# Seven small transfers instead of three, so that the last store counts on the last semaphore waited for

## The chip, the cores and the metric

The kernel runs on 1 core of one Trainium2 chip. Its five engines are TensorE (PE in the profile, its weight loads PEld), VectorE (DVE), ScalarE (ACT), GpSimd (POOL) and SyncE (SP). SP computes nothing here: it starts most transfers between HBM and the on-chip memory. The metric is device time in microseconds (us) of one execution.

## The reference

Two stages over `x` of 4 batches, 11,456 tokens and 128 channels, all in float32.

```python
h = mab(I, x)            # 32 inducing points attend to all tokens of a batch
y = mab(x, h)            # every token attends to the 32 rows of h
xn = y / (norm(y) + 1e-6);  en = emb / (norm(emb) + 1e-6)
logits = xn @ en.T / tau                       # 8 experts
out = max(softmax(logits)) * relu(y @ w1[e]) @ w2[e],   e = argmax(logits)
```

`mab(q, kv)` is softmax(q kv^T / sqrt(128)) kv. Three inputs are small: the inducing points (`ind`, 16 KB), the experts' embeddings (`emb`, 4 KB) and one number, `tau`.

## The kernel before, in words

Each batch is cut into 6 pieces of 1,920 tokens, so there are 24 pieces. A piece is 960 KB in and 960 KB out. For a piece g the program has steps with names: `load g` (transposed layout) and sometimes `loadx g` (plain layout) bring it in, `xt`/`xe` transpose it on the chip where `loadx` does not, `s1`, `e1`, `e1t`, `h` do the first attention, `s2`, `am`, `e2`, `ud`, `w`, `n2`, `ln`, `ex`, `den`, `lg`, `el`, `S`, `v`, `gf` the second one and the gate, `F`, `eg`, `out`, `oe` the output, and `store g` writes it. Steps of a batch (`hd`, `tab`, `vote`, `pick`, `loadw`, `G`, `GT`, `gs`, `gk`, `K`) find its expert and fetch that expert's weights. The first piece is loaded in two halves, `load 0.0` and `load 0.1`; pieces 17, 18, 20, 22 and 23 are written in two halves.

The order of the work is written out by hand. `ORDER` (line 42) is one list of all steps; each engine runs its steps in that order. `AT` (line 99) is a string of digits: each time a step of the list touches a buffer for the first time, the next digit is its place (which of 18 big buffers, which of 8 PSUM banks). `FILL` (line 105) names steps before which TensorE multiplies zeros into a bank that is free: `out 17.1:2:1:w` is one multiplication of 512 columns into bank 2 ahead of `out 17.1`.

**Transfers and semaphores.** Each transfer counts on one of eight semaphores, DMAHW0 to DMAHW7, which are handed out in turn. The order of the turns is about that of the list, SP's and ACT's transfers mixed. Before a transfer may take a semaphore that an earlier one has, its engine waits until the earlier one has landed. So a row `[waits DMAHW3_49]` on a transfer says at once which semaphore it counts on (unless its buffer or the pace of the loads asks for that landing too) and that the transfer eight turns ago has to have landed. SP's loads are also paced: load number n of the list waits for load n - 6.

The three small inputs are started by ACT: `ind` (line 305) one transfer, `small` (line 307) one for `emb` and one for `tau`. With SP's 73 transfers that makes 76.

**The end.** The kernel checks bounds on its own shortcut (`verdict`), reads a count (line 810) and enters a loop (line 812) which repairs batches; the count is 0 here and no pass is made. Leaving that loop, each of the five engines passes the same row of waiting instructions: for DMAHW1 together with DMAHW0, then DMAHW2, DMAHW3, and so on to DMAHW7, then for the engines. After it the engines meet at a barrier, which GpSimd gathers, and a second one.

Of the kernel before, what the change touches and what calls it, by code (L numbers as in the profile page):

```python
# [23 lines left out]
E = 8  # L24
# [14 lines left out]
LOADED = [3, 6, 7, 8, 13, 14, 15, 16, 19, 20, 22]  # L39


ORDER = """load 0.0, load 0.1, ind, small, xt 0.0, s1 0, xt 0.1, xe 0.0, load 1, m1 0, xe 0.1, sha 0, xt 1.0, load 2, xt 1.1,
s1 1, s1 2, en1, en3, xe 1.0, shb 0, shc 0, xe 1.1, shd 0, e1 0, en4, e1t 0, xt 2.1, en5, load 4, xe 2.1, xt 2.0,
xe 2.0, xt 4.1, xt 4.0, en6, e1 1, e1 2, pz 0, e1t 1, py 0, h 0, load 3, s1 3, s1 4, e1t 2, h 1, h 2, e1 4, xe 4.1,
e1t 4, e1 3, xe 4.0, pad 5, e1t 3, load 5, s1 5, e1 5, zc 0, en7, xt 5.0, xt 5.1, loadx 3, load 6, xe 5.0, h 3,
# [50 lines left out]
store 22.0, eg 23.1, verdict.0, verdict.1, verdict.2, verdict.3, out 23.1, oe 22.1.1, store 22.1, verdict.4,  # L96
verdict.5, oe 23.1.0, oe 23.1.1, verdict, store 23.1"""

AT = """0024120363045430065602601011745018109021046abc00d10121324356ef0732g1h7210161000213400045617261a042030111013700
8114c060100463230010013150146003911364102117eh8360710c00216004006133145701011600421000b116240671d1452117502f90  # L100
645610014043141b006400201100016c402601101004509h23156000252410006101342015106200111401158006710262514a6106275c
24000g62111301103460010e02409101216430201301641d103101264130c010100420015062814502610254116211116010426404011g
2064a020416201f14012362460"""

FILL = """xt 0.0:6:17:n, tab 3:1:2:w, out 17.1:2:1:w, out 18.1:0:3:w, out 19:2:1:w, out 21:4:2:w, out 20.0:3:10:w,
out 23.0:5:2:w, out 22.0:5:1:w, ck4 3:6:1:w, out 23.1:7:2:w"""

BY_DVE = (
# [44 lines left out]
class Plan:  # L153
# [5 lines left out]
    def add(self, name, engines, f, reads=(), writes=()):  # L159

        part = lambda a: a if isinstance(a, tuple) else (a, None)
        op = Op(name, engines, f, [part(a) for a in reads], [part(a) for a in writes])
        for key in op.reads + op.writes:
            w, r = self.hist.setdefault(key, [None, []])
            if w is not None and w is not op:
                op.deps.add(w)
        for key in op.writes:
            op.deps.update(x for x in self.hist[key][1] if x is not op)
            self.hist[key] = [op, []]
        for key in op.reads:  # L170
            self.hist[key][1].append(op)
        op.bufs = list(dict.fromkeys(k[0] for k in op.reads + op.writes))
        for b in op.bufs:
            b.left += 1
        self.ops.append(op)
        return op

    def run(self):
        named = {op.name: op for op in self.ops}
        order = [named[n.strip()] for n in ORDER.split(",")]  # L180
        assert len(named) == len(self.ops) == len(order) == len(set(order))
        holds = {(k, s): None for k, n in SLOTS.items() for s in range(n)}
        at, done = iter("".join(AT.split())), set()
        for o in order:
# [17 lines left out]
def tile_attn_moe(ctx: ExitStack, tc: tile.TileContext, xT, xP, xR, indT, emb, tau, w1, w2, aux, outT):  # L202
    nc = tc.nc
# [17 lines left out]
    for kind, shapes in dict(  # L221
# [3 lines left out]
        w=dict(w1=[P, F], w2=[P, 8, C]),  # L225
# [9 lines left out]
    ident, ind, ones, iota = const("ident", [P, P]), const("ind", [P, M]), const("ones", [P, P]), const("iota", [P, E])  # L235
# [3 lines left out]
    en, itau, ess, nrm = const("en", [P, E]), const("itau", [E, 1]), const("ess", [E, P]), const("nrm", [E, 4])  # L239
    emb_sb = const("emb_sb", [E, P])  # L240
# [38 lines left out]
    add = plan.add  # L279
# [22 lines left out]
    cbuf, cnb = Buf("cst"), Buf("cst")  # L302
    enb, tb = Buf("cst"), Buf("cst")

    add("ind", {"ACT": (0.6, 16e3)}, lambda e: [nc.scalar.dma_start(ind, indT)], [], [cnb])

    def load_small(e):
        return [nc.scalar.dma_start(emb_sb, emb), nc.scalar.dma_start(itau, tau.broadcast_to([E, 1]))]

    add("small", {"ACT": (1.0, 5e3)}, load_small, [], [tb])  # L310

    def experts1(e):
# [432 lines left out]
    with tc.manual_schedule():  # L745
        nc.scalar.preload_act_table_set("natural_log_exp_and_others")
        constants()
        hist, last, paced = {}, {}, []
        fills = {n.strip(): (int(s), int(k), w == "w") for n, s, k, w in (x.split(":") for x in FILL.split(",") if x.strip())}
        for op in order:  # L750
            res = []
            for key in (op.reads, op.writes):
                out = []
# [9 lines left out]
            if op.name in fills:  # L763
                s, n, wide = fills[op.name]
                w, r = hist.setdefault(("ps", s), [None, []])
# [4 lines left out]
            for key in reads + writes:  # L770
                w, r = hist.setdefault(key, [None, []])
# [40 lines left out]
    with tc.For_i(0, n_left, 1) as b:  # L812
# [12 lines left out]
        xt, pe = tile_("xt", [P, GW]), tile_("pe", [M, GW])  # L825
        m1, nb1, fx, zc1 = (tile_(n, [M, 1]) for n in ("m1", "nb1", "fx", "zc1"))
# [26 lines left out]
        r1, r2, half, place, at_e = (tile_(n, [GW, 1]) for n in ("r1", "r2", "half", "place", "at_e"))  # L853
# [93 lines left out]
```

## Time and profile before

| | |
|---|---|
| median of 3 runs | 164.43 us (164.41, 164.43, 166.8) |
| the profiled execution's own time | 164.44 us |
| its span, first to last instruction | 162.6 us |
| granted TensorE clock over the span | 0.99 |
| PE, DVE, ACT, POOL busy | 151.5, 122.8, 113.6, 67.8 us |
| moved by transfers | 62.33 MB, 383 GB/s mean |

The span leaves out 1.9 us of the execution's time. A row of a timeline has the start and the length in us, engine, source line, operation, tiles and, in brackets, how long the engine was idle before and what ended the idling. An engine with a q behind its name is its sequencer: transfers being issued, semaphore waits and branches, which do not count as busy. Names such as `big` leave the buffer's number out.

### The profile page before, as it was taken

What the parts mean: (1) busy time and instruction counts of PE and PEld (TensorE: products, weight loads), DVE (VectorE), ACT (ScalarE), POOL (GpSimd) and SP (SyncE); (2) the same over time, 40 slices, a digit from 0 to 9 for tenths busy, and PEclk for the clock granted to TensorE, in tenths of its full rate; (3) what the DMA queues carried; (4) which work ended last, traced back from release to release, by engine and by line L of the source; (5) the groups of instructions that cost most, each with busy time, mean ns of one, the idle gap of its engine ahead of it and who ended that gap; (6) DMA issues with size and microseconds to landing.
All of it is one profiled execution on the core that took longest, in us unless ns stands there. A gap on an engine that the chain in (4) does not pass through costs nothing.

```text
span 162.6 us, 5452 instructions
## 1 busy us (share of the span) xinstructions
PE 151.5 (93%) x2130; PEld 85.3 (52%) x2134; DVE 122.8 (76%) x308; ACT 113.6 (70%) x249; POOL 67.8 (42%) x179
## 2 busy tenths in 40 slices
PE   7999999999999999999999999999999998998720
PEld 5769695335986633546487423658753223233300
DVE  0175743699978789999986598989898989996620
ACT  3239361683985888697678877699968879987740
POOL 8700010116266470524142552942456275775500
PEclk9999999999999999999999999999999999999995
DMA  5999999999999999999999989999999999879972
GB/s 165 428 429 420 429 422 427 407 315 423 422 416 429 423 386 415 425 418 421 429 416 368 403 295 310 381 427 427 416 419 422 322 420 401 343 302 421 405 294 97
DMA packets 10716, 62.33 MB, mean 383 GB/s; under 512 B 1336, under 2 KB 1344, under 8 KB 10688
## 3 DMA queue, kind: packets, MB, share of 16 engines
q1 hardware_dynamic: 10512, 61.94, 94.4%
q8 instruction: 17, 0.28, 0.6%
q14 instruction: 11, 0.09, 0.1%
q10 hardware_dynamic: 176, 0.02, 0.1%
HBM read 38.49 MB, written 23.46 MB: 381 GB/s over the span
## 4 chain that ended last, share of the span: by engine, by line
PE 83%; ACT 9%; POOL 2%; issue 1%; DVE 1%; ACTq 0%; POOLq 0%
PE psum L294 65%; PE psum L404 14%; ACT big L291 5%; PE psum L768 3%; PE psum L366 1%; ACT s L636 1%; POOL Wp L620 1%; ACT gf L653 1%; ACT U L291 1%; ACT E L601 1%; POOL E2g L677 0%; ACT s L637 0%; POOL lg L644 0%; DVE fl L709 0%; POOL chk L482 0%
## 5 line engine op out<-in xcount | busy, mean ns | idle before, releaser
L291 ACT COPY big<-psum 128x960 f32<-128x960 f32 (+4 forms) x71 | 57.4, 845 | 13.9 <-PE psum L294 8.0
L677 POOL TENSOR_TENSOR E2g<-E,F 128x480 f32<-128x480 f32 (+2 forms) x26 | 26.8, 1035 | 15.0 <-DVE F L675 10.7
L294 PE MATMUL psum<-E2g,K 32*128 32x480 f32 (+2 forms) x232 | 27.3, 542 | 1.9 <-ACT big L291 0.9
L294 PE MATMUL psum<-big,E1T 128*32 128x128 f32 x720 | 24.9, 273 | 0.0
L294 PE MATMUL psum<-big,ind 128*32 128x480 f32 x192 | 24.5, 569 | 0.0
L404 PE MATMUL psum<-ident,big 128*128 128x128 f32 x195 | 23.8, 278 | 0.0
L294 PEld LDWEIGHTS psum<-big,E1T 128*32 128x32 f32 x720 | 21.9, 110 | 3.6 <-issue 1.4
L404 PEld LDWEIGHTS psum<-ident,big 128*128 128x128 f32 x195 | 21.8, 143 | 3.3 <-issue 1.6
L294 PE MATMUL psum<-big,hd 128*32 128x480 f32 x192 | 23.3, 571 | 0.0
L294 PE MATMUL psum<-E,tG 64*64 64x480 f32 x96 | 21.1, 571 | 0.2 <-ACT E L601 0.2
L294 PE MATMUL psum<-E,tD 64*64 64x480 f32 x96 | 21.2, 571 | 0.0
L428 ACT ACTIVATE E<-psum,nb 128x480 f32<-128x480 f32 x24 | 15.8, 661 | 7.6 <-PE psum L294 4.2
L449 DVE STREAM_TRANSPOSE E1T<-E 128x480 f32<-128x480 f32 x24 | 15.9, 664 | 4.9 <-PE psum L294 3.2
L620 POOL TENSOR_TENSOR Wp<-U,E 128x480 f32<-128x480 f32 x9 | 10.8, 1207 | 14.8 <-ACT U L291 14.7
L601 ACT ACTIVATE E<-psum,nb 128x480 f32<-128x480 f32 x24 | 15.2, 664 | 2.5 <-DVE am L593 2.5
L675 DVE STREAM_TRANSPOSE F<-gf 128x480 f32<-128x480 f32 (+2 forms) x29 | 16.4, 572 | 0.3
L593 DVE TENSOR_REDUCE am<-psum 128x1 f32<-128x480 f32 x24 | 15.1, 638 | 1.4 <-PE psum L294 1.3
L291 DVE COPY big<-psum 128x960 f32<-128x960 f32 (+2 forms) x13 | 14.9, 1147 | 1.0 <-PE psum L404 1.0
L294 PEld LDWEIGHTS psum<-E2g,K 32*128 32x128 f32 x232 | 9.3, 183 | 11.0 <-POOL E2g L677 3.9
L630 DVE TRANSPOSE_TENSOR_REDUCE n<-Wp 128x30 f32<-128x960 f32 x12 | 13.8, 1154 | 0.7 <-POOL Wp L620 0.6
L294 PEld LDWEIGHTS psum<-E,tG 64*64 64x64 f32 x96 | 6.5, 132 | 13.6 <-issue 6.6
L644 POOL TENSOR_TENSOR lg<-DT,den 128x240 f32<-128x240 f32 x12 | 7.7, 640 | 6.7 <-DVE den L642 6.5
(137 smaller groups left out, 188.5 us busy)
## 6 DMA issues: line engine op xcount, KB each, us to landing
big<-in_xT SPq DMA_DIRECT2D x19, 960.0 KB, 11.2
out<-big SPq DMA_DIRECT2D x17, 960.0 KB, 8.9
big<-in_xP SPq DMA_DIRECT2D x11, 960.0 KB, 10.8
w<-in_w SPq DMA_DIRECT2D x8, 512.0 KB, 4.9
big<-in_xT SPq DMA_DIRECT2D x4, 928.0 KB, 11.8
out<-big SPq DMA_DIRECT2D x5, 512.0 KB, 4.3
out<-big SPq DMA_DIRECT2D x2, 928.0 KB, 6.1
out<-big SPq DMA_DIRECT2D x3, 448.0 KB, 3.2
```

Source lines behind the costliest of these rows:

```text
L291: return nc.scalar.copy(out, in_) if e == "ACT" else ENG[e].tensor_copy(out, in_)
L294: return nc.tensor.matmul(out, lhsT=lhsT, rhs=rhs, start=start, stop=stop)
L404: return [nc.tensor.transpose(flat(tp)[:, 128 * (q - q0):128 * (q - q0) + 128], v(q), ident) for q in range(q0, q1)]
L428: return [nc.scalar.activation(E1s if one else ap(e1), src, AF.Exp, bias=bt.t("nb")[:, 0:1], scale=SCALE, accum_out=bt.t("zk")[:, k:k + 1])]
L449: add(f"e1t {g}", {"DVE": 0.59}, lambda e: [nc.vector.transpose(ap(e1t), ap(e1))], [e1], [e1t])
L593: add(f"am {g}", {"DVE": 0.57}, lambda e, ps=ps, k=k: [v.tensor_reduce(t("am")[:, k:k + 1], ap(ps)[:, :W], AX.X, ALU.max, apply_absolute_v ...
L601: add(f"e2 {g}", {"ACT": 0.56}, lambda e, ps=ps, a=a: [nc.scalar.activation(ap(e2)[:, a], ap(ps)[:, :W], AF.Exp, bias=t("nb")[:, 1:2], sca ...
L620: return [ENG[e].tensor_tensor(ap(wp)[:, a], src(), ap(e2)[:, at(a)], ALU.mult)]
L630: add("n2 " + nm, {"DVE": 1.08}, lambda e: [v.tensor_reduce(fl2(u("n2")), ap(wp).rearrange("p a (q i) -> p (a q) i", i=32), AX.X, ALU.add, ...
L644: add("lg " + nm, {"POOL": 0.64}, lambda e: [gp.tensor_tensor(u("lg"), dv(), u("den").rearrange("p a q -> p q a").unsqueeze(3).broadcast_t ...
L675: add(f"F {nm}", {"DVE": 0.09 + 0.51 * part}, lambda e, a=a, f=f, q0=q0, q1=q1: [v.transpose(ap(f).rearrange("p (q i) -> p q i", i=32)[:, ...
L677: add(f"eg {nm}", {"POOL": 0.06 + 1.15 * part, "DVE": 0.2 + 0.54 * part}, lambda e, a=a, fs=fs, e2g=e2g, c0=c0, c1=c1: [ENG[e].tensor_tens ...
```

## The change

`ind` becomes two transfers of 64 partitions, `emb` three (rows 0 to 3, 4 and 5, 6 and 7), `tau` two (partitions 0 to 3 and 4 to 7). ACT then starts seven transfers instead of three, and the program has 80. In the list the first loads stand ahead of `small`. `AT` gives some pieces each other's big buffers (the first three; 19 and 20; `loadx 22` and 23; the outputs of 19 and 21, and that of 22), and no other PSUM bank to any step. One multiplication of zeros before `out 17.1` goes, two before `G 3` come.

```diff
-ORDER = """load 0.0, load 0.1, ind, small, xt 0.0, s1 0, xt 0.1, xe 0.0, load 1, m1 0, xe 0.1, sha 0, xt 1.0, load 2, xt 1.1,
+ORDER = """load 0.0, ind, load 0.1, load 1, load 2, small, xt 0.0, s1 0, xt 0.1, xe 0.0, m1 0, xe 0.1, sha 0, xt 1.0, xt 1.1,
...
-FILL = """xt 0.0:6:17:n, tab 3:1:2:w, out 17.1:2:1:w, out 18.1:0:3:w, out 19:2:1:w, out 21:4:2:w, out 20.0:3:10:w,
+FILL = """xt 0.0:6:17:n, tab 3:1:2:w, G 3:1:2:w, out 18.1:0:3:w, out 19:2:1:w, out 21:4:2:w, out 20.0:3:10:w, out 23.0:5:2:w,
...
-    add("ind", {"ACT": (0.6, 16e3)}, lambda e: [nc.scalar.dma_start(ind, indT)], [], [cnb])
+    add("ind", {"ACT": (0.6, 16e3)}, lambda e: [nc.scalar.dma_start(ind[r:r + 64], indT[r:r + 64]) for r in (0, 64)], [], [cnb])
...
-        return [nc.scalar.dma_start(emb_sb, emb), nc.scalar.dma_start(itau, tau.broadcast_to([E, 1]))]
+        return [nc.scalar.dma_start(emb_sb[r0:r1], emb[r0:r1]) for r0, r1 in ((0, 4), (4, 6), (6, 8))] + [nc.scalar.dma_start(itau[r:r + 4], tau.broadcast_to([4, 1])) for r in (0, 4)]
```

SP at the start of the program, before (`big_65` is piece 0, `big_67` piece 1, `big_68` piece 2, `big_70` piece 4, `big_72` piece 3, `big_74` piece 5):

```order
L383 DMA big_65<-in_xT 128x896
L383 DMA big_65<-in_xT 128x1024
L386 DMA big_67<-in_xT 128x1920
L386 DMA big_68<-in_xT 128x1920
L386 DMA big_70<-in_xT 128x1920
L386 DMA big_72<-in_xT 128x1920 [waits DMAHW0_49]
L386 DMA big_74<-in_xT 128x1856 [waits DMAHW1_49]
L396 DMA big_75<-in_xP 128x1920 [waits DMAHW2_49]
L386 DMA big_76<-in_xT 128x1920 [waits DMAHW5_49,DMAHW3_49]
```

And with the change (piece 1 is now in `big_66`, piece 2 in `big_67`):

```order
L383 DMA big_65<-in_xT 128x896
L383 DMA big_65<-in_xT 128x1024
L386 DMA big_66<-in_xT 128x1920
L386 DMA big_67<-in_xT 128x1920 [waits DMAHW2_49]
L386 DMA big_70<-in_xT 128x1920 [waits DMAHW3_49]
L386 DMA big_72<-in_xT 128x1920 [waits DMAHW4_49]
L386 DMA big_74<-in_xT 128x1856 [waits DMAHW5_49,DMAHW0_49]
L396 DMA big_75<-in_xP 128x1920 [waits DMAHW6_49]
L386 DMA big_76<-in_xT 128x1920 [waits DMAHW7_49]
```

The load of piece 2, which waited for nothing, now waits for DMAHW2, the semaphore of `load 0.1`; those of pieces 4, 3 and 5 wait for small transfers. On ACT the first `tau` transfer waits for DMAHW0 (`load 0.0`), the second for DMAHW1 (the first half of `ind`).

SP at the end, the last stores before (`big_80` is piece 23, `big_66` piece 22):

```order
L690 DMA out<-big_80 128x1024 [waits DMAHW0_49,Activation_49]
L690 DMA out<-big_66 128x1024 [waits DMAHW1_49,Activation_49]
L810 TENSOR_LOAD ni [waits DVE_49]
L810 ISA x2
L690 DMA out<-big_66 128x896 [waits DMAHW2_49,Activation_49]
L690 DMA out<-big_80 128x832 [waits DMAHW3_49,Activation_49]
```

And with the change (piece 22 is now in `big_76`):

```order
L690 DMA out<-big_80 128x1024 [waits DMAHW4_49,Activation_49]
L690 DMA out<-big_76 128x1024 [waits DMAHW5_49,Activation_49]
L810 TENSOR_LOAD ni [waits DVE_49]
L810 ISA x2
L690 DMA out<-big_76 128x896 [waits DMAHW6_49,Activation_49]
L690 DMA out<-big_80 128x832 [waits DMAHW7_49,Activation_49]
```

The last store counted on DMAHW3 and counts on DMAHW7 now. The row of waits at the loop's exit is the same in both programs.

PE around `G 3` (line 294, `psum<-w_149,hd_113`) and `out 17.1` (`E2g_93`, 224 columns), the difference:

```order
+L768 LDWEIGHTS zwide
+L768 MATMUL psum<-zwide 128x512
+L768 LDWEIGHTS zwide
+L768 MATMUL psum<-zwide 128x512
 L294 MATMUL psum<-w_149,hd_113 32x256 x4
 L294 MATMUL psum<-E2g_93,K_144 128x256 x4
```

Two zero multiplications stand ahead of `G 3`; the one ahead of `out 17.1` (four rows on) is gone.

## Rows read from the trace of the kernel before

**Rows 1.** The page: busy us (share of the span) and instructions of each engine.

```profile
PE 151.5 (93%) x2130; PEld 85.3 (52%) x2134; DVE 122.8 (76%) x308; ACT 113.6 (70%) x249; POOL 67.8 (42%) x179
```

**Rows 2.** Stretches: busy us (instructions) of PE, PEld, DVE, ACT, POOL; clock, DMA share, GB/s.

```profile
0.00:1.50 1.50, 0.45 (x3) 0.33 (x4) 0.36 (x4) 0.77 (x1) 0.89 (x13) 1.00 0.00 0
1.50:2.00 0.50, 0.50 (x4) 0.38 (x3) 0.00 (x0) 0.50 (x1) 0.50 (x4) 1.00 0.76 115
12.00:120.00 108.00, 107.95 (x1715) 65.53 (x1713) 88.04 (x214) 80.19 (x182) 41.16 (x84) 1.00 1.00 403
131.00:143.00 12.00, 11.13 (x131) 3.89 (x129) 11.15 (x25) 11.70 (x28) 8.94 (x14) 1.00 0.92 379
160.25:160.75 0.50, 0.00 (x0) 0.00 (x0) 0.00 (x0) 0.00 (x0) 0.00 (x0) 0.50 0.00 0
```

**Rows 3.** Timeline of the end: start and length of SP's last store.

```profile
156.79 0.38 SPq L690 DMA_DIRECT2D out<-big  x1
```

**Rows 4.** SP's own waits from 157.2 us on: total us, times, longest us.

```profile
SPq L812 <- DMA out<-big: 2.9, 3, 1.4
```

**Rows 5.** Line 812 from 160.80 us on: count, ns min/median/max, first and last start.

```profile
L812 PEldq EVENT_SEMAPHORE  x6: 51/51/51, 160.8 to 161.5; - x6
```

**Rows 6.** Line 812 from 161.03 to 161.42 us: the middle waits.

```profile
L812 PEldq EVENT_SEMAPHORE  x4: 51/51/51, 161.0 to 161.3; - x4
```

**Rows 7.** Line 942 from 161.3 to 162.0 us: the arrivals at the first barrier.

```profile
L942 POOLq EVENT_SEMAPHORE  x2: 17/17/17, 161.8 to 161.9; - x2
L942 DVEq DRAIN  x1: 17/17/17, 161.6 to 161.6; - x1
L942 PEldq DRAIN  x1: 8/8/8, 161.8 to 161.8; - x1
```

**Rows 8.** The halves of piece 0: issue, and us from issue to landing.

```profile
L383 SPq DMA_DIRECT2D big<-in_xT x2: 390/406/421, 0.7 to 1.2; - x2
...
DMA to landing us min/median/max: 3.5/3.9/4.3
```

**Rows 9.** Loads of pieces 1 and 2, the same columns.

```profile
L386 SPq DMA_DIRECT2D big<-in_xT x2: 424/434/445, 1.7 to 2.1; - x2
...
DMA to landing us min/median/max: 6.1/7.1/8.0
```

**Rows 10.** Timeline of PEld and DVE: first use of piece 2, and of the embeddings.

```profile
10.13 0.13 PEld L294 LDWEIGHTS psum<-big,ind 128*32 128x32 f32 x4 [0.28 <-DMA big<-in_xT]
...
9.20 0.27 DVE L313 TENSOR_TENSOR ess<-emb_sb 8x128 f32<-8x128 f32 x1
```

**Rows 11.** Timeline of ACT at the start.

```profile
1.19 0.58 ACTq L308 DMA_DIRECT2D emb_sb<-in_emb  x1
6.09 0.91 ACT L291 COPY big<-psum 128x896 f32<-128x896 f32 x1 [4.08 <-PE psum L404]
```

**Rows 12.** Timeline of PE from 134 us: `G 3`, `out 17.1`, three zero multiplications.

```profile
134.44 0.61 PE L294 MATMUL psum<-w,hd 128*32 128x256 f32 x8
...
137.94 0.66 PE L294 MATMUL psum<-E2g,K 32*128 32x224 f32 x8 [0.62 <-ACT big L291]
...
141.61 0.82 PE L768 MATMUL psum<-zwide 128*128 128x512 bf16 x3
```

**Rows 13.** Timeline of DVE and ACT there: `GT 3`, `S 18`, `el 18`.

```profile
135.31 0.40 DVE L532 STREAM_TRANSPOSE GT<-psum 128x256 f32<-128x256 f32 x1
...
136.76 0.43 DVE L648 TENSOR_REDUCE sum<-ex 128x30 f32<-128x270 f32 x1
...
136.32 0.41 ACT L646 ACTIVATE ex<-lg 128x240 f32<-128x240 f32 x1
```

**Rows 14.** SP's timeline at the loads of pieces 20 and 19.

```profile
73.99 1.56 SPq L386 DMA_DIRECT2D big<-in_xT  x2
```

**Rows 15.** The transfer before those, `loadx 16`: issue and landing.

```profile
L396 SPq DMA_DIRECT2D big<-in_xP x1: 328/328/328, 73.6 to 73.6; - x1
...
DMA to landing us min/median/max: 6.6/6.6/6.6
```

More of the change, by code (lines that the diff above doesn't have):

```diff
@@ L97 @@
 verdict.5, oe 23.1.0, oe 23.1.1, verdict, store 23.1"""
[L99 to L103, printed above, removed]
-FILL = """xt 0.0:6:17:n, tab 3:1:2:w, out 17.1:2:1:w, out 18.1:0:3:w, out 19:2:1:w, out 21:4:2:w, out 20.0:3:10:w,
-out 23.0:5:2:w, out 22.0:5:1:w, ck4 3:6:1:w, out 23.1:7:2:w"""
+AT = """0120243036045430065602601011745018109021046abc00d10121324356ef0732g1h7210163000213400045617261a042030111013700
+8114c060100462130010013150146003911364102117eh8360710c00216004006132145701011600421000b116240671d3452117502f90
+64561001404b1412006400201100016c402601101004509h23156000252410006103342015106200111401158006710262514a6101675c
+24000g62111301103460010e02409101216430201301641d103101264130c010100420015062814502610254116211111010426g040114
+2064a020416201f140b2362460"""
+FILL = """xt 0.0:6:17:n, tab 3:1:2:w, G 3:1:2:w, out 18.1:0:3:w, out 19:2:1:w, out 21:4:2:w, out 20.0:3:10:w, out 23.0:5:2:w,
+out 22.0:5:1:w, ck4 3:6:1:w, out 23.1:7:2:w"""
 BY_DVE = (
```

## The prediction, made before the run

> **What bounds the kernel now.** I read the busy times first, then stretches of the span, then the two ends row by row, because the change is at the two ends. TensorE is busy 151.5 us [rows 1], and from 12 to 120 us 107.95 of 108.00 us [rows 2]: whatever starts it later in the first 12 us comes out at the end, since there is no idle time to make it up in. The transfers are as full in that stretch, DMA share 1.00 at 403 GB/s [rows 2]. From 131 us ScalarE is the fullest, 11.70 of 12.00 us against 11.13 for TensorE [rows 2]. The end is neither. SP issues the last store at 156.79 us [rows 3], and in what is left it waits three times for stores, 2.9 us in all [rows 4]. Each engine has six waiting instructions of the loop's exit from 160.8 us on; on TensorE the first starts at 160.8, when the last store has landed, and the sixth at 161.5 us [rows 5]. TensorE comes to the barrier at 161.8 us, VectorE at 161.6, and GpSimd's first barrier instruction starts at 161.8 too [rows 7]. So behind the last landing the time is TensorE stepping over waits that have long been met.
>
> **What the change takes away at the end.** The waits are passed in the order DMAHW1 with 0, 2, 3, 4, 5, 6, 7, engines. The last store counted on DMAHW3, so the instructions for 4, 5, 6, 7 and the engines' own came after its landing: with the one that waits for it that is the six seen. Counting on DMAHW7, only the engines' own comes after. Four instructions per engine then run before the landing, beside the transfer. Their price on TensorE: four of them start from 161.0 to 161.3 us [rows 6], three steps of 0.1 us, and the next is the sixth, at 161.5 [rows 5]; that puts four steps, from the second to the sixth, at 0.4 to 0.5 us. The two bounds: four times the instruction's own 51 ns [rows 5], 0.20 us, and four of the five steps of the whole row, 0.7 x 4/5 = 0.56 us [rows 5]. I take **0.42 us**, by the steps. VectorE, at 161.6, has the same four fewer and would come well before TensorE's new 161.4 [rows 7]; so the barrier moves with TensorE.
>
> **The start: seven issues on ScalarE.** The longest of its issues now is 0.58 us [rows 11]; seven at no more than that take 4.1 us from 0.7 on, to 4.8. The two `tau` transfers at their end also wait for `load 0.0` (landed at 0.7 + 3.5 = 4.2 us, rows 8) and for the first half of `ind`, a wait of about that size; two issues from 4.2 on end at 5.4 at the latest. ScalarE's first work starts at 6.09 us after 4.08 us of idling for TensorE [rows 11], which covers them with 0.7 us to spare; each us beyond that would put off the first copy by as much. The embeddings are first read at 9.20 us [rows 10], more than 5 us after their last issue. I cost all of this at nothing.
>
> **The start: loads wait for small transfers.** Piece 2 was issued at 2.1 us and landed 8.0 us later, at 10.1 [rows 9]; TensorE picks it up at 10.13 us with the transfer named as what it waited for [rows 10]. So a later landing counts fully. Now SP holds it until `load 0.1` has landed, 1.2 + 4.3 = 5.5 us [rows 8]; everything SP issues afterwards stands behind it. How early must it be issued? Piece 1, ahead of it, lands at 1.7 + 6.1 = 7.8 us [rows 9], and 2.3 us lie between the landings of 1 and 2, which is 960 KB at the rate of full queues: piece 2's time is set by its turn, not by its issue. At the very start the first issue is at 0.7 us [rows 8], the engines of the transfers are idle until 1.5 and at 0.76 from there to 2.0 us [rows 2]: about 1.0 us from issue to flow, 1.3 at most. Issued at 5.5 it can flow by 6.5 to 6.8 us; piece 1's data ends some 0.5 us before its landing (at the end of the program nothing flows from 160.25 us on, and the landing is at 160.8, rows 2, 5), so piece 2 is wanted at about 7.3. The margin is 0.5 to 0.8 us and I cost the term at **nothing**, with -0.1 (fewer transfers in front of the small ones) and +0.5 us (flow a microsecond later than at the start) as its bounds. Pieces 4, 3 and 5 then follow at about 0.4 us each and wait for the second half of `ind` and two parts of `emb`, issued before 3.5 us. What is late next, were piece 2 on time, is the load of piece 6, which waits for the last part of `emb` and, as before, for piece 1 at 7.8.
>
> A rule speaks against splitting: the Trainium skill ("DMA: Bandwidth & Descriptors", section "Anatomy of one DMA") gives a transfer a fixed cost of about 2.0 us whatever its size, and its section on bandwidth calls transfers under 64 KB descriptor-dominated. By it four more would cost up to 8 us if each stood in line on the path, and the sum would be near 172 us. By the rows they stand beside 4.08 us of idling, and the sum is as above.
>
> **Buffers.** Pieces 20 and 19 exchange places, so piece 20 now waits for what held up 19. The two are issued in 1.56 us from 73.99 [rows 14], so 20 slips by at most 1.2 us, to 75.2. The transfer in front lands at 73.6 + 6.6 = 80.2 us [rows 15]; by the 1.3 us from issue to flow it would have to slip past 78 to be late. Nothing. `loadx 22` and piece 23 exchange in the same way, with queues as full. The late outputs only get other free buffers.
>
> **Zero multiplications.** Three of them take 0.82 us [rows 12], so each up to 0.27. The one that goes stood ahead of `out 17.1`, which idles 0.62 us for ScalarE [rows 12]: it leaves idle time, nothing else. The two that come push `G 3` by up to 0.55 us, its end from 134.44 + 0.61 = 135.05 to 135.60 us [rows 12]. `GT 3` starts on VectorE at 135.31 [rows 13], so it would be 0.29 late, and what follows it on VectorE with it, until `S 18` at 136.76, which waits for ScalarE's `el 18` until 136.73 anyway [rows 13]; between the end of `GT 3` at 135.71 and there stand two steps of about its 0.40 us, so some 0.2 us of the lateness is room. Left over is 0 to 0.29 us; I take **0**, since ScalarE is the full engine there [rows 2].
>
> **The sum.** -0.42 + 0 + 0 + 0. Against the profiled execution's own 164.44 us (span 162.6 and 1.9 outside it) that is 164.02, and that execution is 0.01 above the median of the runs: **164.0 us**. With the terms' bounds, -0.56 - 0.1 and -0.20 + 0.29, it is 163.8 to 164.5; the +0.5 us of a late piece 2 is a rival's.
>
> **The rivals.**
> - *Piece 2 runs dry* (slower than before). If the landing of `load 0.1`, with more small transfers round it, or the start of the flow is a microsecond late, the transfer engines idle between pieces 1 and 2 and TensorE loses that time for good. It decides from 0.42 us on, that is when piece 2 lands later than 10.5 us. At 11.1 us it gives 164.44 - 0.42 + 1.0 = 165.0. For it: the margin is short and TensorE does wait for this landing [rows 10]. Against: the flow began 1.0 us behind the first issue. 0.12.
> - *No gain to see*: `G 3`'s zeros and steps on VectorE take back most of it, or another engine is nearly as late at the barrier as TensorE: 164.2 to 164.5. VectorE at 161.6 moves too, which is against it. 0.14.
> - *The change does not do what it says*: the order of the waits at the exit is not the order of the landings. The last landing was followed by exactly the six instructions expected, so 0.03, at 164.4.
> - *More than the end*: with only three large loads issued at the start the small ones and `load 0.1` land sooner and TensorE's first steps close up: 163.3 to 163.8. TensorE starts when its own zeros are done, so 0.06.
> - *A mishap of microseconds*: the four added transfers land one behind the other ahead of the loads (four times the 3.5 us of rows 8 is 14 us, 178 us in all), or the granted clock, 1.00 from 131 to 143 us [rows 2], falls where a zero multiplication is missing: 168 us and more. 0.02.
>
> **The numbers.** The forecast, 163.8 to 164.2, has 0.63. With the no-gain cases, the better one in part and the slower one as far as 0.7 us of loss, the range **163.6 to 164.7** holds over 0.8. Two per cent, about what a measurement of this kernel can tell from no change, is 3.3 us here: faster by more has 0.01, slower by more 0.02 with the last rival, the rest 0.97 is within.
>
> **What would show it.** At the end: on TensorE two instructions of the exit's row from the last landing on, not six, and 1.0 us or less from that landing to GpSimd's first barrier instruction's end, 0.4 less than now. At the start: piece 2 issued near 5.5 us and landed near 10.1, ScalarE's first copy near 6.1. At 135 us: `GT 3` up to 0.3 us later, `S 18` at its place relative to its neighbours. The prediction is wrong if piece 2 lands after 10.5 us, if SP's last store is issued more than 0.2 us from where it was, or if TensorE is not the last at the barrier.

## The result: 167.1 us instead of 164.5, outside the predicted range

| | before | with the change |
|---|---|---|
| median of 14 runs each | 164.47 us (164.27 to 166.8) | 167.1 us (164.43 to 168.14) |
| the profiled execution | 164.44 us, span 162.6 | 167.07 us, span 165.2 |
| last landing to the end of the span | 1.76 us | 1.24 us |

The ratio of the compared runs is 1.0058, 95% interval 1.0033 to 1.0083, so the change is slower, where 0.997 was forecast. That ratio leaves out every run more than 1.5% above a kernel's fastest, which here are 9 of 14 with the change and 1 of 14 before, at the same granted clock (0.98 to 0.99) as the rest, so I give medians of all runs beside it (167.1 / 164.47 = 1.016). A median of 167.1 is 2.4 us above the predicted range. The two kernels differ by less than 2%, as predicted.

**The end did what was predicted.** The page's busy row of the changed kernel, answering [rows 1], SP's last store [rows 3] and its waits from 160.3 us on [rows 4]:

```profile
PE 154.2 (93%) x2131; PEld 84.8 (51%) x2135; DVE 122.9 (74%) x308; ACT 113.6 (69%) x249; POOL 67.6 (41%) x179
```

```profile
159.94 0.38 SPq L690 DMA_DIRECT2D out<-big  x1
```

```profile
SPq L812 <- DMA out<-big: 2.2, 2, 1.5
```

From the last landing (163.95 us) on, line 812 on TensorE, answering [rows 5]; then line 942, answering [rows 7]:

```profile
L812 PEldq EVENT_SEMAPHORE  x2: 51/51/51, 164.0 to 164.1; - x2
```

```profile
L942 DVEq DRAIN  x2: 10/14/17, 164.4 to 164.7; - x2
L942 PEldq DRAIN  x2: 8/8/8, 164.4 to 164.8; - x2
L942 POOLq EVENT_SEMAPHORE  x2: 17/17/17, 164.5 to 164.6; - x2
```

Two waits are left of six, and TensorE reaches the barrier 0.5 us after the landing, where it took 1.0. But the last store itself is issued 3.15 us later than before: the loss lies ahead of it.

**Where the time went.** I matched each copy, activation and reduction of ScalarE and VectorE with the same one of before, by their order, and took the difference of the starts. The columns are the shift near that time of the program before, in us; the last two are from the last landing to the end of the span, and the span:

```
                    6     14     22     32    110    145   landing-end    span
changed kernel    0.62   1.31   2.50   3.35   3.12   3.16      1.24      165.19
the same again    0.31   1.13   1.13   1.13   0.90   0.94      1.24      162.96
before             -      -      -      -      -      -        1.76      162.56
```

The loss is made in four steps in the first 30 us, and then nothing is given back, as a full TensorE cannot. (The fall of 0.23 near 90 us is a wait that only the profile of before has; it is in none of the others.)

The first step is the clock's, not the change's. These are the seven transposes of the first half of piece 0, of before first:

```profile
4.65 1.41 PE L404 MATMUL psum<-ident,big 128*128 128x128 f32 x7
```

```profile
4.65 1.70 PE L404 MATMUL psum<-ident,big 128*128 128x128 f32 x7
```

TensorE has multiplied zeros since 1.05 us. The profile's records of the granted clock, at 1.00, begin at 5.6 us before and at 7.0 us here; ahead of that moment the transposes start 0.21 us apart, behind it 0.11, so the clock rises there from the lower to the higher of its two levels. (The stretches of [rows 2] show 1.00 ahead of it too, where there is no record.) Over the sixteen profiles of this document the records begin anywhere from 3.7 to 7.0 us. Three kernels of the experiments where they begin at 6.7 to 6.9 us (four spare transfers; `ind` in halves, alone and with the late load) are 0.48 to 0.57 us late near 8 us as well.

The loads of pieces 1 and 2, issue and us to landing, answering [rows 9]; then TensorE's waits in its timeline:

```profile
L386 SPq DMA_DIRECT2D big<-in_xT x2: 328/376/424, 1.7 to 5.6; - x2
...
DMA to landing us min/median/max: 5.9/6.7/7.5
```

```profile
9.23 1.86 PE L404 MATMUL psum<-ident,big 128*128 128x128 f32 x15 [0.48 <-DMA big<-in_xT]
...
21.78 1.00 PE L294 MATMUL psum<-big,ind 128*32 128x480 f32 x5 [0.18 <-issue]
...
28.99 0.48 PE L294 MATMUL psum<-rhs,hsb 128*32 128x160 f32 x8 [0.65 <-issue]
```

Piece 1 lands at 1.65 + 7.53 = 9.18 us (7.79 before), piece 2 at 5.61 + 5.90 = 11.51 (10.09 before, predicted 10.1). TensorE waits at 9.2 us for piece 1, which hides most of the wait for piece 2. At 21.8 and 29.0 us it waits for nothing that the profile names, and that is two of the three microseconds. (The brackets show only a part of these two stalls: the multiplication ahead of each is counted as busy for its full modelled length, and from start to start they are 0.75 and 1.09 us.) Stretches of both kernels, columns as in [rows 2]; of before first:

```profile
7.00:8.50 1.50, 1.50 (x14) 1.50 (x15) 1.10 (x2) 0.00 (x0) 0.42 (x5) 1.00 1.02 430
```

```profile
7.00:8.50 1.50, 1.50 (x17) 0.94 (x9) 0.66 (x1) 0.29 (x1) 0.39 (x4) 1.00 0.96 328
```

The transfer engines are busy in both, 0.96 against 1.02, but move 328 instead of 430 GB/s: they do not run dry, their packets take longer. In the packet records a row of 7,680 bytes takes 0.29 us; between 7.0 and 8.3 us of the changed kernel, where piece 2 begins, fourteen take 0.36 to 1.18 us. Before has none over 0.35 us there. Over all profiles, those with the load of piece 2 issued at 5.6 to 5.8 us have 11 to 17 packets over 0.35 us in that stretch and move 312 to 359 GB/s, eight of eight; the eight others have none to four and move 394 to 440.

### The profile page after: what moved, and what is told of

Its sections match the earlier page's. It is cut to its first block, busy times and chain, and to the rows that moved or that the text cites. A ratio compares the mean times of both kernels' runs of the same rounds, so it can differ in the third digit from the quotient of the medians.

```text
span 165.2 us, 5456 instructions
## 1 busy us (share of the span) xinstructions
PE 154.2 (93%) x2131; PEld 84.8 (51%) x2135; DVE 122.9 (74%) x308; ACT 113.6 (69%) x249; POOL 67.6 (41%) x179
## 4 chain that ended last, share of the span: by engine, by line
PE 83%; DMA 5%; ACT 3%; DVE 3%; issue 2%; POOL 1%; SPq 0%; ACTq 0%; POOLq 0%
PE psum L294 67%; PE psum L404 13%; DMA big<-in_xT 5%; ACT big L291 2%; PE psum L768 1%; PE psum L366 1%; DVE F L675 0%; SPq L383 0%; DVE sum L648 0%; POOL E2g L677 0%; ACT gf L653 0%; DVE gf L652 0%; ACT E L601 0%; POOL v L649 0%; ACT s L636 0%
## 5 line engine op out<-in xcount | busy, mean ns | idle before, releaser
L294 PE MATMUL psum<-big,ind 128*32 128x480 f32 x192 | 25.6, 576 | 0.2 <-issue 0.2
L294 PEld LDWEIGHTS psum<-big,ind 128*32 128x32 f32 x192 | 6.7, 110 | 7.0 <-issue 4.2
## 6 DMA issues: line engine op xcount, KB each, us to landing
big<-in_xP SPq DMA_DIRECT2D x11, 960.0 KB, 11.5
```

Source lines behind the costliest of these rows:

```text
L294: return nc.tensor.matmul(out, lhsT=lhsT, rhs=rhs, start=start, stop=stop)
```

## The experiments

Kernels compared together shared a chip and the runs of before (medians 164.37 to 164.5, 15 to 29 runs each, of them 1 or 2 over 166 us). Runs over 166 us are counted for each kernel, since most scatter between 164 and 168. A ratio is that of the compared runs, with its 95% interval. A transfer of 128 partitions lands in sixteen parts, which the expectations call rings; a piece is whole with the last of them. What an instruction block is stands under 3.

**1. The end alone.** First by stores in halves, which misled:

```diff
-[nc.sync.dma_start(outT[b, :, ...], ap(o)[:, t0:t1])]
+# pieces 3, 6, 9, 12: two transfers of 64 partitions
+[nc.sync.dma_start(outT[b, r:r + 64, ...], ap(o)[r:r + 64, t0:t1]) for r in (0, 64)]
```

> The kernel before with its three small transfers; the stores of pieces 3, 6, 9 and 12 go out as two transfers of 64 partitions each, so there are 80 transfers and the last store counts on DMAHW7, while the first 30 us issue exactly what they issued before. If the loss of the changed kernel lies in its start and the end is worth what the prediction said, 163.9 to 164.1 us, with the waits of the loop's exit passed ahead of the last landing. If the count at the end is worth nothing by itself, 164.4 to 164.5. If halving transfers costs by itself, wherever it is done, 165 or more.

166.0 us median of 12 (164.13 to 167.75), ratio 1.0037 [0.9995, 1.008]. The start is as before and the end as it should be (1.24 us), but new time is lost near 136 us. Line 506 there is the load of a batch's weights, issued at 126.5 us, and who waited for it:

```profile
L506 SPq DMA_DIRECT2D w<-in_w x1: 1278/1278/1278, 126.5 to 126.5; - x1
...
  PE psum L296: 1.9, 1
...
DMA to landing us min/median/max: 10.2/10.2/10.2
```

It landed after 10.2 us, 4.2 before. The sixteen parts of a transfer landed up to 6.4 us apart from 118 us on, at most 2.2 in the kernel before. So it says nothing on the end. Then by four tiny transfers that come late enough to touch nothing:

```diff
+add("spare", {"ACT": (1.0, 5e3)}, lambda e: [nc.scalar.dma_start(spare[r:r + 2], emb[r:r + 2]) for r in (0, 2, 4, 6)], [], [Buf("cst")])
-xt 0.1, xe 0.0, load 1, m1 0,
+xt 0.1, xe 0.0, load 1, spare, m1 0,
```

> The kernel before; its first eight transfers stay as they are, and four more follow on ACT behind the first copy of piece 0 (near 6.5 us): emb once more, in four transfers of two rows, into a tile that nobody reads. 80 transfers, the last store counts on DMAHW7, the load of piece 2 waits for nothing. If the end is worth what the prediction said (0.42 us) and the changed kernel's loss lies in the late load of piece 2: 164.0 to 164.2, no ring of piece 1 late, no TensorE wait at an instruction block. If the end's gain needs something else of the change: 164.4 to 164.6. If tiny transfers on ACT cost by themselves: 165 or more.

**163.96 us** median of 7 (163.77 to 164.24), ratio **0.9963 [0.995, 0.9977]**, none over 166: the best median of all kernels here. Loads of pieces 1 and 2, and the exit's waits behind the landing at 161.01 us:

```profile
L389 SPq DMA_DIRECT2D big<-in_xT x2: 424/436/448, 1.6 to 2.1; - x2
...
DMA to landing us min/median/max: 6.3/7.2/8.1
```

```profile
L815 PEldq EVENT_SEMAPHORE  x2: 51/51/51, 161.0 to 161.1; - x2
```

Piece 2 is issued at 2.1 and lands at 10.26 us; the end is 1.24 us. The end is worth what the prediction said: 0.5 us of the median, 0.52 at the end of the span. Over all profiles the time from the last landing to the end goes with the semaphore that the last store counts on: 1.76 us on DMAHW3 (before, and the kernels with the late load alone), 1.55 and 1.66 on DMAHW4 (`ind` in halves), 1.34 on DMAHW6, 1.24 on DMAHW7, on the average 0.13 us a step.

**2. The late load alone, the small transfers alone.**

```diff
+if op.name == "load 2":
+    tc.add_manual_dep(op.insts[0].ins, paced[1].insts[-1].ins.name, ...)   # load 0.1
```

> The kernel before, three small transfers, 76 in all; only the load of piece 2 waits for load 0.1 and is issued at some 5.5 us instead of 2.1, and the loads behind it on SP follow. Theory A (the late loads are the cause: their first packets are slow, and TensorE's instruction blocks come late): no ring of piece 1 is late, but packets of piece 2 and later take over 350 ns instead of 291, the first instruction blocks start 4 to 5 us after they are asked for and TensorE stands at them: 165.5 to 166.5 us. Theory B (the five small transfers on ACT disturb the rings of the loads): 164.4 to 164.6.

165.74 us median of 12 (164.63 to 167.54), 6 over 166, ratio 1.0044 [1.0004, 1.0084]. The load of piece 2, then TensorE's waits:

```profile
L386 SPq DMA_DIRECT2D big<-in_xT x1: 328/328/328, 5.8 to 5.8; - x1
...
DMA to landing us min/median/max: 5.4/5.4/5.4
```

```profile
11.23 1.01 PE L294 MATMUL psum<-big,ind 128*32 128x480 f32 x8 [0.32 <-DMA big<-in_xT]
...
21.26 1.00 PE L294 MATMUL psum<-big,ind 128*32 128x480 f32 x5 [0.25 <-issue]
...
29.01 0.48 PE L294 MATMUL psum<-rhs,hsb 128*32 128x160 f32 x8 [1.19 <-issue]
```

One wait added to the kernel before makes the same picture: piece 2 at 11.2 us, TensorE waiting for it (work shifted by 0.80 us), and the two nameless stalls at the same instructions (1.26 and 1.40 more). Piece 1 is not late.

Five small transfers without the late load (`emb` and `tau` divided as in the change, the rest as before):

> The kernel before with its own list, emb in three and tau in two parts as in the change, ind in one: 79 transfers. The load of piece 2 now waits only for ind (4.4 us, 1.1 us earlier than in the changed kernel), that of piece 4 for load 0.1 (5.5). Theory B (small transfers disturb the rings): one ring of piece 1 lands over 1 us after the others, TensorE waits for it near 8.5 us, 166 to 167 us. Theory A (late loads): piece 2 flows on time, 164.1 to 164.8 (the end gains some 0.3).

164.07 us median of 12 (163.81 to 167.04), 1 over 166, ratio 0.9949 [0.9918, 0.9981]. The theory that small transfers disturb the rings falls: piece 1 is whole at 8.01 us. But the profiled run, 164.81, is one of the slower ones, and there piece 2, issued at 4.63 us, came at 11.53 and TensorE waited for it, which I had not expected:

```profile
11.57 1.01 PE L294 MATMUL psum<-big,ind 128*32 128x480 f32 x8 [0.72 <-DMA big<-in_xT]
```

The same with `tau` in three, by which the load of piece 2 waits for `load 0.1` once more:

> emb in three and tau in three transfers, ind in one, before's list: 80 transfers, the last store counts on DMAHW7; the load of piece 2 waits for load 0.1 as in the changed kernel (5.5 us; in the kernel with tau in two it waited for ind, 4.6 us, and the median was 164.07). If that one wait decides: late instruction blocks at TensorE in most runs, median 165 to 166.3, runs from 164 to 167.5. If the number of small transfers or ind's halves decide instead: 163.9 to 164.2 as with tau in two.

164.71 us median of 9 (164.05 to 168.32), 4 over 166, ratio 1.0035 [0.9996, 1.0073]. TensorE in its profile:

```profile
11.51 1.01 PE L294 MATMUL psum<-big,ind 128*32 128x480 f32 x8 [0.57 <-DMA big<-in_xT]
```

Its median is below what I expected and no block is late in its profile, but between it and the one above stands one more transfer of 8 bytes and one turn: issue of piece 2 at 5.7 instead of 4.6 us, with 0.64 us of median and 4 of 9 runs over 166 instead of 1 of 12. `ind` in halves, without and with the late load (`paced[1]` as above):

```diff
-[nc.scalar.dma_start(ind, indT)]
+[nc.scalar.dma_start(ind[r:r + 64], indT[r:r + 64]) for r in (0, 64)]
```

> The kernel before with ind in two halves of 64 partitions and nothing else: 77 transfers; the load of piece 2 waits for nothing, that of piece 4 for load 0.0 (4.2 us); the last store counts on DMAHW4. Theory C (ind in halves makes one ring of piece 1 land over 1 us after the others, as in both profiles of the changed kernel, 9.2 and 9.0 us): piece 1's last ring near 9 us, TensorE waits some 0.7 us near 8.5 us, 165.2 to 165.6. Against it (the late ring comes with the late load of piece 2): piece 1 whole by 8.2 us, 164.3 to 164.5.

164.95 us median of 12 (164.28 to 166.85), 2 over 166, ratio 1.001 [0.998, 1.004]; piece 1 whole at 8.0 us. The median lies between the two expectations, 0.46 us above that of before, and the ratio does not tell it from no change.

> The kernel before with ind in two halves and the load of piece 2 waiting for load 0.1; emb and tau in one transfer each. In both profiles of the changed kernel one ring of piece 1 landed near 9.1 us, over 0.9 us after the rest; in the kernels with either of the two edits alone none did. If the two together make it: piece 1's last ring after 8.8 us. If it needs the five small transfers of emb and tau too: by 8.3 us. Time: as late load alone, 165 to 167.5.

165.36 us median of 8 (164.86 to 168.53), 3 over 166, ratio 1.0065 [1.0021, 1.011]; piece 1 whole at 7.95 us, piece 2 at 11.9. So a late ring of piece 1 needs more than `ind`'s halves and the late load.

**3. What TensorE stands at.** The two stalls are before TensorE's 449th and 705th recorded instruction (counted from 0) in both kernels that have them, 256 apart. The page has a queue of its own, 17 packets of 0.28 MB in all, 16 KB each:

```profile
q8 instruction: 17, 0.28, 0.6%
```

TensorE has 4,356 records of matrix multiplications, weight loads and waits; the first packet comes behind the 193rd, and one for every 256 records from there on makes 17. The Trainium skill ("Runtime: NRT & Kernel Launch", section "Instruction fetch mechanics") says that an engine refills its instructions in blocks of 16 KiB or 256 instructions over a DMA queue of its own, "mostly hidden". Block and count agree with this trace; "mostly hidden" holds for thirteen of the sixteen profiles, not for the three with stalls at 449 and 705. To see whether the stall goes with the count or with the step, I moved the steps against the count:

```diff
-FILL = """xt 0.0:6:17:n, tab 3:1:2:w, G 3:1:2:w, ...
+FILL = """xt 0.0:6:9:w, tab 3:1:2:w, G 3:1:2:w, ...
+v.memset(zwide, 0.0)    # on VectorE ahead of zero, instead of on GpSimd
```

> The changed kernel with 9 zero multiplications of 512 columns instead of 17 of 256 ahead of the first transposes (and the tile of zeros for them set by VectorE): about the same time on TensorE, 16 instructions fewer, everything behind them the same. If TensorE stands for blocks of 256 instructions, a stall (where this run has one) is again just before its 449th or 705th recorded instruction, which is now 16 instructions later in the program: inside the 15 transposes of piece 5 instead of in s1 5, and inside the multiplications of hd instead of the first with rhs. If it stands for data of a step, it is before the same steps as in the changed kernel. 164.5 to 168 us.

166.04 us, without such a stall in this run: TensorE waited 0.70 us for the second half of `ind`, which landed at 7.20 us, and the last store took 1.0 us longer. The same kernel once more:

> The same kernel as the one with 9 wide zero multiplications, for a second profile, since not every run has such a stall; the same two expectations.

169.33 us, with both. TensorE there:

```profile
22.54 0.55 PE L404 MATMUL psum<-ident,big 128*128 128x128 f32 x3
23.67 1.47 PE L404 MATMUL psum<-ident,big 128*128 128x128 f32 x12 [0.58 <-issue]
...
28.56 0.62 PE L294 MATMUL psum<-rhs,hsb 128*32 128x160 f32 x8
30.00 1.01 PE L294 MATMUL psum<-big,ind 128*32 128x480 f32 x8 [0.82 <-issue]
```

The stalls are again before records 449 and 705, and now inside the transposes of piece 5, between the third and the fourth, and behind the multiplications with `rhs` instead of before them, sixteen records on as the count demands (I had named `hd` as the step there). The three transposes that ran read the same landed piece as the twelve that waited, so it is no data. TensorE stood for its own instructions; one run shows the places moved. The packet records say when such a block is read; "entered" is the start of the record 256 ahead of a block's end, and TensorE stands from the start of the last record of a block to that of the next:

```
                 piece 2   block read 0        block read 1        TensorE stands
                 issued    entered  started    entered  started    at the ends of them
before            2.12      12.96    14.74      19.14    22.92      0     0
four spare        2.12      13.45    16.54      19.64    22.66      0     0
changed, again    5.67      14.09    15.21      20.28    23.27      0     0
changed           5.61      14.27    19.48      21.78    26.68      0.75  1.09
late load         5.80      13.69    18.88      21.26    26.65      0.82  1.64
9 wide zeros, b   5.76      16.16    21.33      23.67    27.79      0.86  1.12
```

A read takes 0.96 us and starts 1.1 to 3.8 us after it could in the runs without stalls, 4.1 to 5.4 us in those with them. These first two blocks last some 6.2 us of work, so a read 3.8 us late is covered and one 5.2 us late is not. At all six stalls TensorE goes on 1.24 to 1.43 us after its read has ended, which ties each stall to its read. By these numbers a start up to some 3.9 us late fits into 6.2 us (an estimate: 6.2 - 0.96 - 1.35); in the last row the second block lasts 5.2 us, and there 4.1 us was too late. The profile counts these reads among the queues of the same sixteen transfer engines as the loads. The Trainium skill ("DMA: Bandwidth & Descriptors", section "Queues, rings and completion order") says that a transfer engine takes turns between its queues packet by packet; no run here shows how many packets a read waited for.

The mirror of this test, 34 instructions more on the kernel with the late load:

> The kernel before with the load of piece 2 waiting for load 0.1, and 34 zero multiplications of 128 columns instead of 17 of 256 ahead of the first transposes: TensorE works about as long, with 34 instructions more. In two kernels TensorE stood just before its 449th and 705th recorded instruction, 256 apart. If it waits there for blocks of instructions that come late, a stall stands again before instruction 449 or 705, now 34 instructions earlier in the program (in the multiplications with E1T ahead of s1 5, and in s1 7 or 6 ahead of those with rhs); if it waits for data that a step needs, it stands before the same steps as there (fourth multiplication of s1 5, the first with rhs). 165 to 167.5 us either way.

166.71 us median of 4 (165.99 to 167.26), ratio 1.0123 [1.0093, 1.0153]. Its profile has no stall before records 449 and 705, so it tells nothing on the place; TensorE waits for pieces 2 and 3 instead (0.42 and 0.53 us). What it has, with 4,394 records, is the queue's row with one block more (by the count above it would be 17 still; why the last one is read here stays open):

```profile
q8 instruction: 18, 0.29, 0.6%
```

The last read now runs at 160.6 us, beside the last store, which lands 5.0 us after its issue. With the 9 wide zeros the last read falls there too (160.2 and 161.4 us), and the store takes 5.0 and 5.6 us. It takes 4.0 in all others but the kernel with halved stores (6.1) and that with `ind` alone in halves (4.7).

**4. The change, undone by one edit at a time.** First the changed kernel once more:

> The changed kernel once more, for a second profile and more times: 14 times of it lay between 164.4 and 168.1 with a median of 167.1. If the late ring of piece 1 and the late instruction blocks of its profile are its rule, they stand in this profile too and the median is near 167; if they are chance, a profile near 164.5 has neither, and the difference between both profiles names what each costs.

166.78 us median of 6 (164.84 to 168.12), 5 over 166, ratio 1.0134 [1.0072, 1.0197]. The profiled run took 164.84: piece 1 late (9.00 us) and piece 2 too (11.29), but the blocks in time. TensorE at piece 1:

```profile
9.04 1.86 PE L404 MATMUL psum<-ident,big 128*128 128x128 f32 x15 [0.59 <-DMA big<-in_xT]
```

So the late pieces cost 0.8 us here (shift 0.31 to 1.13), and of the 2.2 us between both profiles the blocks are 2.04 (1.31 to 3.35) and the first transposes, which the clock decides, 0.3. Then `ind` in one transfer again, all else as in the change:

> The changed kernel with one edit undone: ind in one transfer. 79 transfers, so the last store counts on DMAHW6, and every turn behind ind comes one earlier: the load of piece 2 waits for ind (4.4 us) and not for load 0.1 (5.6). If that one turn decides: 163.9 to 164.3 median, most runs under 164.5. If the change's other parts (its list, its buffers, the zero multiplications, five transfers of emb and tau) cost anything: 165 or more.

164.25 us median of 12 (163.83 to 167.15), 3 over 166, ratio 0.9975 [0.9945, 1.0005]. Load of piece 2:

```profile
L386 SPq DMA_DIRECT2D big<-in_xT x1: 327/327/327, 4.6 to 4.6; - x1
...
DMA to landing us min/median/max: 5.7/5.7/5.7
```

With `ind` whole and the load thereby one turn earlier, 2.5 to 2.9 us of the median are back. Last, all seven transfers, with the five of `emb` and `tau`, or `tau`'s two alone, behind the first copy:

```diff
-load 1, load 2, small, xt 0.0, s1 0, xt 0.1, xe 0.0, m1 0,
+load 1, load 2, xt 0.0, s1 0, xt 0.1, xe 0.0, small, m1 0,          # all five late
+load 1, load 2, small, xt 0.0, s1 0, xt 0.1, xe 0.0, tau, m1 0,     # tau's two late
```

> The changed kernel with all its seven small transfers, 80 in all and the last store on DMAHW7, but emb's and tau's five stand behind the first copy of piece 0 on ACT (issued near 6.5 us), so the load of piece 2 waits for nothing and is issued near 2.1 us. If the late load of piece 2 is the whole loss: 163.9 to 164.4 with every run under 165 (ind in halves may still cost some tenths at the first scores). If ind's halves or the number of small transfers cost by themselves: 165 and more, runs scattered up to 167.

165.95 us median of 6 (164.69 to 166.41), 3 over 166, ratio 1.0087 [1.0059, 1.0116]. The kernel does not test what it was meant to: `emb` now comes late itself, and VectorE waits for it:

```profile
12.02 0.28 DVE L313 TENSOR_TENSOR ess<-emb_sb 8x128 f32<-8x128 f32 x1 [2.67 <-DMA emb_sb<-in_emb]
```

One thing it does show: the load of piece 2 is issued at 2.1 us, and still the last ring of piece 1 lands at 8.71 us and TensorE waits 0.56 us for it. So that ring needs no late load.

> The changed kernel with its seven small transfers and 80 in all, but tau's two stand behind the first copy of piece 0 on ACT (near 6.5 us; tau is wanted near 13.8), so the load of piece 2 waits only for load 0.0 and is issued near 4.4 us, and emb is no later than before. If the late load of piece 2 is the whole loss: 163.9 to 164.3. If ind's halves beside emb's parts make one ring of piece 1 land near 9 us by themselves: that ring again, TensorE waits some 0.6 to 0.8 us for it, 164.5 to 165.0.

164.63 us median of 12 (163.76 to 165.71), none over 166, ratio 1.0002 [0.9982, 1.0022]. Piece 2 was issued at 4.46 us and landed at 10.53; no late blocks. In its profile the second half of `ind` landed at 6.79 us, and the first scores waited:

```profile
6.92 1.01 PE L294 MATMUL psum<-big,ind 128*32 128x480 f32 x8 [1.39 <-DMA ind<-in_indT]
```

In the eight profiles with `ind` in halves its second half lands at 5.8 to 7.2 us, `ind` whole at 4.4 to 4.8, and TensorE waits for the half in four of them (0.19 to 1.39 us). So `ind` in halves can cost time by itself, beside the turn that it takes. As a median of some tenths, here and in the kernel that has only that edit, it is not clear of the noise.

## Why the prediction was wrong, step by step

- *The end, -0.42 us (0.20 to 0.56)*: right. 1.76 to 1.24 us is -0.52, and six waits became two.
- *Seven issues on ScalarE, 0*: right. The last ends at 4.95 us; the first copy starts at 6.39 instead of 6.09, but so it does with three early transfers in the kernel with four spare ones. The first seven transposes end between 5.45 and 6.64 us from profile to profile, with the clock and without a tie to the change. The price that was weighed against splitting, up to 8 us for four more transfers, did not come: four tiny transfers more go with 163.96 us. The section of the Trainium skill from which the prediction took it ("DMA: Bandwidth & Descriptors", "Anatomy of one DMA") describes transfers that GpSimd starts, and these are ScalarE's.
- *Loads wait for small transfers, "I cost the term at nothing"*: **this step failed.** SP's issue at 5.6 us was predicted to 0.1 us. The conclusion, "piece 2's time is set by its turn, not by its issue", with a margin of 0.5 to 0.8 us, was wrong: issued at 5.6 to 5.8 us it landed at 11.1 to 12.8, in eight profiles, instead of 10.1. Two of the prediction's own signs of being wrong came with it: piece 2 after 10.5 us, and the last store 3.15 us from its place. I had asked when the first byte would flow. From 7 us on bytes did flow, but at 328 GB/s: the packets with which a load begins were slow when it had been issued shortly before its turn. It is not the loads behind it that slow them: in the first run of the kernel with 9 wide zeros the next load is issued at 7.22 us only, and twelve packets of piece 2 that start from 7.15 to 7.79 us take 0.36 to 0.89 us all the same. Nor did pieces 4, 3 and 5 follow at 0.4 us each, but at 5.98, 6.75 and 7.42 us. Issued at 4.5 to 4.6 us it landed at 10.4, 10.5 and 11.5, so the edge is about there; issued at 2.1 us, at 10.1 to 10.5 (11.0 once, behind a late piece 1).
- *The rival "piece 2 runs dry"* named this, with 0.12, the landing from which it decides (10.5 us) and 165.0 us. That is the size of the runs without late blocks (164.84), its mechanism right but for the word dry. The rest, 2.0 and 2.7 us in the two profiles that the shifts above were read from, was in no term and no rival, and is the larger part of the loss: late blocks of TensorE's instructions. The page's row of the instruction queue had been there to read; I took TensorE's program as free.
- *Buffers, 0*: right; the shift stays between 3.1 and 3.4 us from 30 to 130 us. *Zero multiplications, 0 (to 0.29)*: right, 0.05 us near 135 us in every kernel that has them.
- The sum without the failed step is about what the runs without it show: 163.96 with a start left alone, 164.25 with the change less `ind`'s halves.

**How much is shown, and what stays open.** The late load alone costs 1.2 us of median (165.74), `ind`'s halves alone 0.5 (164.95, not clear of noise), both 0.9 to 1.0 (165.36, against 164.37); the five others cost nothing (164.07, with 0.4 of the end in it). The whole change costs 2.3 to 2.6 with the end's gain in it, and without the late load 0.2 or less (164.63, 164.25, where no or a quarter of the runs is over 166 us; 16 of 20 are with it). So the late load is needed for the whole of the loss, but the parts do not add up to it. One thing stands only there: in five of the six profiles with both `ind` in halves and `emb` and `tau` divided a ring of piece 1 lands at 8.71 to 9.18 us, and in four of them TensorE waits 0.5 to 0.6 us for it; in the sixth (`tau` late) it is 8.22, in the ten other profiles 7.79 to 8.19. Which of the parts together bring it was not settled; the late load is not needed for it. Nor was it settled what decides whether a block is read 1 or 5 us late: late blocks stand in three of the eight profiles with the late load and in none of the eight without it, and how the one brings the other is not shown.

## What to carry to other kernels

Before you divide or add a transfer, list which later transfers take over its semaphores, and for what each then has to wait: one turn more moved a 960 KB load from 4.6 to 5.7 us, and with that a median 0.4 us better than before became one 0.2 worse (`tau` in two parts, in three); in the whole change, with `ind` in halves too, it was a loss of over 2. A load needs its place in the queue well ahead of its turn, which here came at about 7.3 us: issued 1.5 to 1.7 us ahead it was late in eight profiles of eight, 2.7 us ahead in one of three; where a count has to be filled up, add something tiny and late that nothing waits for. In a kernel that fills both TensorE and the queues, look for stalls with "issue" as the releaser at a fixed distance in instructions: here they were the program itself arriving late.

## What was not expected of the hardware

- TensorE reads its program in blocks of 256 instructions (16 KB) over the transfer engines during the run, mostly 0.9 to 1.0 us long each, and stood up to 1.6 us for one; where a block was read beside the last store, the store's landing came 1.0 to 1.6 us later, in three profiles of three (two others came 0.7 and 2.1 us later without one).
- A load that was issued 1.5 to 1.7 us ahead of its turn kept the transfer engines busy (share 0.96) at three quarters of their rate (328 against 430 GB/s), with first packets of up to 1.2 us instead of 0.29.
- With four stores of 960 KB as two halves of 64 partitions each, the sixteen parts of later transfers landed up to 6.4 us apart instead of 2.2, and a load of weights took 10.2 instead of 4.2 us, in one profile.
- TensorE's clock rose to its higher level anywhere from 3.7 to 7.0 us in kernels that multiply the same zeros from 1.05 us on, and that alone shifts the first 8 us of work by some tenths from run to run.
